# Second half of the channel weights converted in ScalarE's order behind channel items, and two passes for three batches instead of two

## The chip, the core and the metric

One core of a Trainium2 chip runs the whole program. TensorE (PE) multiplies, VectorE (DVE), ScalarE (ACT) and GpSimd (POOL) do elementwise work, SyncE (SP) issues the DMAs. Each engine takes its instructions in one fixed order and waits on semaphores where an operand is not ready. The metric is device time in microseconds (us), lower is better.

## What is computed

Attention with rotated q and k over 4 batches, 8 heads, 576 positions, then two mixing layers. The last layer (moe2) is the one the change touches:

```python
h = np.maximum(xt @ w_tok1, 0.0) @ w_tok2      # along the 576 positions
u = x + h.transpose(0, 2, 1)
h2 = np.maximum(u @ w_ch1, 0.0) @ w_ch2        # 512 -> 1536 -> 512 channels
return u + h2
```

The layer before it makes `x = sigmoid(xr @ w_r) * (relu(xk @ w_k)**2 @ w_v)`. The weights come as 64-bit floats, so each weight tile is first turned into 32-bit words on the chip and then split into a high and a low part; each product is three matmuls (high by high, high by low, low by high).

## The kernel before

The program has an order that a scheduler makes from priorities and from its own reckoning of when operands are ready; the order in which the source emits instructions is only its starting point. Three stages at the end matter here.

**Gates and tokens.** `gate_gen(b)` makes, for each batch and each half of 288 positions, four tiles `f` (DVE, L956) and splits them into `xs` (ACT and POOL), then sixteen groups of three matmuls into `rp`, a sigmoid `q` on ACT and a product `y` on POOL. `tok_gen(b)` transposes `y` into `trp`, copies it to `ytk` (high part on ACT, low part on DVE), multiplies by `w_tok1` into `t1p`, splits the result `h` and multiplies by `w_tok2` into `t2p`, which DVE adds to `y`. The tokens of the last batch (3) run beside the first channel items.

**Channels.** `ch_gen` works in *items*: one item is one tile of 128 of the 1536 channels for one half of one batch, so there are 8 chunks x 12 = 96 items. An item has 12 matmuls into `c1p`, a `hs` high part (ACT, relu with a scale), a float copy `ht` of the same (DVE, L1120), the low part `hs = ht - hs` (POOL, L109), and, two items later (`LAG = 2`), 12 matmuls into four accumulators `co`. Items of one chunk and one half of the channels make a run of `HALF = 6` items. `TWICE = 2` says that the first two batches (4 chunks) are done in two passes: first the lower six channel tiles of all four chunks (blocks with `hs = (0,)`), then the upper six (`(1,)`). The remaining chunks take both halves in one block (`(0, 1)`). At a block's end DVE empties the four `co` tiles (L1142), and for a first pass leaves the partial sum in `sums`. Before a block, `chain` finds its scale (DVE, with one matmul `mp` over the partitions) and `split` makes `uhl` from `u` (four times ACT L80 and DVE L1095).

**Weight conversion.** `Conv` takes weight tiles in pairs through four stages: DMA of `words`, `cv` on ACT (L213), three integer operations and a row maximum on DVE (L217, L218, L220, L225), and `parts`: high on ACT (L80 into `parts`), low on DVE (L238). `conv2` holds the lower half of `w_ch1` (8 tiles of 384 columns); `conv3`, here `cv3`, the upper half of `w_ch1` (8 tiles of 384) and the upper half of `w_ch2` (6 tiles of 512): 14 tiles, needed from the first `(1,)` block on. Its steps are emitted in the loop of the channel stage.

Of the kernel before, what the change touches and what calls it, by code (L numbers as in the profile page):

```python
# [7 lines left out]
F32 = mybir.dt.float32  # L8
# [4 lines left out]
ALU = mybir.AluOpType  # L13
# [21 lines left out]

KVN = 5

CW, HALF, TWICE = DCH // 2, KC // 2, 2

PACE, STEP, REST = (24, 28), 1, 8  # L40

# [28 lines left out]
def body(tc, kin, qin, vw, tabs, ident, mu, w_k, w_v, w_r, w_t1, w_t2, w_c1, w_c2, out):  # L70
# [41 lines left out]
    with ctx:  # L112
# [68 lines left out]
        class Conv:  # L181


            def __init__(self, cv, weights, name, load=None, low="P", room=None):
                self.cv, self.name, self.load, self.low, self.room = cv, name, load, low, room
                self.q = [(w, i) for w in weights for i in range(len(w.srcs))]
                if weights[-1].raw:
                    self.q[:0] = [None] * (len(self.q) % 2)
                self.n, self.words, self.t = 0, {}, {}
# [4 lines left out]
            def stage(self, j, i):  # L194
# [15 lines left out]
                if j == 1:  # L210
                    v = self.t[i] = self.cv()[:, :w]
                    x = hw if wide else self.words[i][:, :w]
                    act.activation(out=v.bitcast(F32), in_=x.bitcast(F32), func=AF.Copy, scale=REBIAS if wide else 1.0)  # L213
                elif j == 2 and wide:
                    v = self.t[i]
                    m = self.room()[:, :w] if self.room else v
# [792 lines left out]
        c2_b = c2_part(HALF, KC)  # L1009
        for nm, n in (("ytk", 1), ("h1", 2), ("uhl", 2), ("hs", 3), ("ht", 2), ("st", 2), ("top", 1)):  # L1010
            M[nm] = top("m_" + nm, n)
        cv, cv3 = Conv(cv_t, c1_w[:1], "conv2", low="D"), Conv(cv_t, [c1_w[1], c2_b], "conv3", low="D")
        def all_max(m):

            p = tps("mp")
# [16 lines left out]
        def ch_gen():  # L1032
# [12 lines left out]

            def part(i):
                b, c = chunks[blocks[i][0]]
                if b not in sums:
                    sums[b] = P["xT"].tile([128, KD, S + 1], F32, tag="xT", name="sums")
                return sums[b][:, :, c * HS:(c + 1) * HS]  # L1050

            def chain(i, k):

# [48 lines left out]
            for n in range(len(items) + LAG):  # L1102
                if n < len(items):
                    i, o, kf = items[n]
                    x = n // HALF
                    last_half = o == blocks[i][1][-1]
                    if kf == 0:
                        chain(i, 0)
                        chain(i, 1)
                        split(x)  # L1110
                    uhl = u16[i, o]
                    p = c1_p.tile([128, 512], F32, tag="c1", name="c1p")
                    for kk in range(KD):
                        mm3(p[:, 0:HS], c1_w[o][kk], kf, uhl[:, kk], kk == 0, kk == KD - 1)
                    j = HALF * o + kf - HALF * blocks[i][1][0]
                    g = tops[blocks[i][1]][1][:, j:j + 1]
                    h = M["hs"].tile([128, 2, HS], F16, tag="hs", name="hs")
                    f = M["ht"].tile([128, HS], F32, tag="ht", name="ht")
                    act.activation(out=h[:, 0], in_=p[:, 0:HS], func=AF.Relu, scale=g)  # L1119
                    dve.tensor_scalar(out=f, in0=p[:, 0:HS], scalar1=g, scalar2=0.0, op0=ALU.mult, op1=ALU.max)  # L1120
                    tt(LOW, h[:, 1], f, h[:, 0], ALU.subtract)
                    hs_of[n] = h
                    if last_half and kf in (0, 2):
                        chain(i + 1, kf // 2)
                    if kf == 4:
                        split(x + 1)
                    yield 12
                if n >= LAG:
                    i, o, kf = items[n - LAG]
                    h = hs_of.pop(n - LAG)  # L1130
                    begin, end = kf == 0 and o == blocks[i][1][0], kf == HALF - 1 and o == blocks[i][1][-1]
                    w, l = c2_at[HALF * o + kf]
                    for m in range(KD):
                        if begin:
                            co_of[m] = co_p.tile([128, 512], F32, tag="co", name="co")
                        mm3(co_of[m][:, 0:HS], w[l], m, h, begin, end)
                    if end:
                        e = row_of[i][:, 5 * KD + 3:]
                        final = blocks[i][1] != (0,)
                        for m in range(KD):  # L1140
                            u = cols(i)[:, m]
                            dve.scalar_tensor_tensor(out=u if final else part(i)[:, m], in0=co_of[m][:, 0:HS], scalar=e,  # L1142
                                                     in1=part(i)[:, m] if blocks[i][1] == (1,) else u, op0=ALU.mult,
                                                     op1=ALU.add)
                        if final:
                            b, c = chunks[blocks[i][0]]
                            sp.dma_start(out[b, c], cols(i))
                    yield 12

        n = 0  # L1150
        while B - 1 not in g_done or B - 2 not in u_done or not cv.done():
# [3 lines left out]
            n += 1  # L1155
            if n % STEP == 0 and not cv.done():
                cv.step()
        ch = Stream(ch_gen())
        ch.advance(1)
        tok.advance(8)  # L1160
# [5 lines left out]
        while not ch.done:  # L1166
            ch.advance(24)
            tok.advance(REST)
            n += 1
            if n % 2 == 0 and not cv3.done():  # L1170
                cv3.step()
        mx.close()
        mw.close()
# [63 lines left out]
```

## Time and profile before

| | us |
|---|---|
| median of 3 runs | 961.42 (959.79 to 962.22) |
| the profiled execution | 953.36 |
| its span, first to last instruction | 951.5 |
| PE busy over the span | 859.0 (90%) |
| DVE busy | 653.4 (69%) |
| ACT busy | 505.0 (53%) |
| POOL busy | 481.1 (51%) |

The span is measured on one execution with the hardware profiler; 1.9 us of its time lie outside the span. All stretches below are in us from the span's start.

### The profile page before, as it was taken

What the parts mean: (1) busy time and instruction counts of PE and PEld (TensorE: products, weight loads), DVE (VectorE), ACT (ScalarE), POOL (GpSimd) and SP (SyncE); (2) the same over time, 40 slices, a digit from 0 to 9 for tenths busy, and PEclk for the clock granted to TensorE, in tenths of its full rate; (3) what the DMA queues carried; (4) which work ended last, traced back from release to release, by engine and by line L of the source; (5) the groups of instructions that cost most, each with busy time, mean ns of one, the idle gap of its engine ahead of it and who ended that gap; (6) DMA issues with size and microseconds to landing.
All of it is one profiled execution on the core that took longest, in us unless ns stands there. A gap on an engine that the chain in (4) does not pass through costs nothing.

```text
span 951.5 us, 18563 instructions
## 1 busy us (share of the span) xinstructions
PE 859.0 (90%) x6870; PEld 751.6 (79%) x6870; DVE 653.4 (69%) x1471; ACT 505.0 (53%) x1121; POOL 481.1 (51%) x512
## 2 busy tenths in 40 slices
PE   3899988897887988997799899999999999999997
PEld 2889977776776877786699898897887888878876
DVE  5898578777698787784997899885545455344332
ACT  2787657767677777784556575653322223223221
POOL 7998568779677765352643354451122222222221
PEclk9999979899999999999999999999999999999999
DMA  8784268898799986889435634100000000000000
GB/s 266 228 273 152 83 138 188 166 198 190 180 173 183 202 164 137 149 169 297 172 120 174 192 118 139 45 2 1 1 1 2 25 26 26 26 25 2 25 26 25
DMA packets 167786, 112.05 MB, mean 118 GB/s; under 512 B 132368, under 2 KB 146832, under 8 KB 167184
## 3 DMA queue, kind: packets, MB, share of 16 engines
q1 hardware_dynamic: 167696, 110.87, 46.7%
q8 instruction: 54, 0.88, 0.4%
q14 instruction: 36, 0.29, 0.1%
HBM read 60.90 MB, written 14.16 MB: 79 GB/s over the span
## 4 chain that ended last, share of the span: by engine, by line
PE 42%; DVE 8%; ACT 3%; issue 2%; DMA 2%; POOL 1%; SPq 0%; DVEq 0%; ACTq 0%; POOLq 0%
PE c1p L712 5%; PE co L712 5%; PE c1p L713 5%; PE c1p L714 5%; PE co L713 5%; PE co L714 5%; DVE cv L218 2%; DVE cv L220 1%; DMA vd<-vt 1%; PE rp L713 1%; PE rp L714 1%; PE rp L712 1%; PE vp L712 1%; PE vp L713 1%; PE vp L714 1%
## 5 line engine op out<-in xcount | busy, mean ns | idle before, releaser
L109 POOL TENSOR_TENSOR hs<-ht,hs 128x288 f16<-128x288 f32 x96 | 71.3, 744 | 231.6 <-DVE ht L1120 195.3
L1119 ACT ACTIVATE hs<-c1p,top 128x288 f16<-128x288 f32 x96 | 47.8, 500 | 194.9 <-PE c1p L714 194.9
L1120 DVE TENSOR_SCALAR ht<-c1p,top 128x288 f32<-128x288 f32 x96 | 49.5, 516 | 119.3 <-ACT hs L1119 118.2
L444 DVE TENSOR_REDUCE nm<-S 128x1 f32<-128x576 f32 x144 | 104.0, 749 | 20.4 <-PE S L431 20.3
L714 PE MATMUL c1p<-uhl,parts 128*128 128x288 f16 x384 | 109.7, 286 | 0.0
L713 PE MATMUL c1p<-uhl,parts 128*128 128x288 f16 x384 | 109.7, 286 | 0.0
L712 PE MATMUL c1p<-uhl,parts 128*128 128x288 f16 x384 | 109.5, 286 | 0.0
L713 PE MATMUL co<-hs,parts 128*128 128x288 f16 x384 | 108.9, 286 | 0.0
L714 PE MATMUL co<-hs,parts 128*128 128x288 f16 x384 | 108.9, 286 | 0.0
L712 PE MATMUL co<-hs,parts 128*128 128x288 f16 x384 | 106.1, 286 | 0.4 <-ACT hs L1119 0.4
L712 PE MATMUL kp<-xs,parts 128*128 128x288 f32 x256 | 81.6, 324 | 21.5 <-ACT t L777 17.1
L431 PE MATMUL S<-kq 64*128 64x288 f32 (+1 forms) x696 | 75.9, 323 | 22.6 <-ACT kq L78 11.3
L712 PEld LDWEIGHTS <-parts 128*128 128x128 f16 x768 | 75.0, 98 | 19.4 <-issue 0.6
L713 PEld LDWEIGHTS <-parts 128*128 128x128 f16 x768 | 75.1, 98 | 19.0 <-issue 0.2
L714 PEld LDWEIGHTS <-parts 128*128 128x128 f16 x768 | 75.2, 98 | 18.9
L431 PEld LDWEIGHTS S<-kq 64*128 64x128 f32 (+1 forms) x696 | 60.1, 198 | 34.4 <-ACT kq L78 11.3
L109 POOL TENSOR_TENSOR q<-t 128x288 f32<-128x288 f32 x64 | 49.2, 771 | 74.2 <-ACT t L777 71.1
L713 PE MATMUL vp<-k,parts 128*128 128x288 f32 x256 | 78.8, 309 | 5.0 <-POOL k L109 4.9
L712 PE MATMUL vp<-k,parts 128*128 128x288 f32 x256 | 79.6, 314 | 4.0 <-ACT t L777 2.2
L713 PE MATMUL kp<-xs,parts 128*128 128x288 f32 x256 | 78.2, 306 | 0.3 <-POOL xs L109 0.2
L714 PE MATMUL vp<-k,parts 128*128 128x288 f32 x256 | 77.6, 304 | 0.0
L714 PE MATMUL kp<-xs,parts 128*128 128x288 f32 x256 | 77.5, 304 | 0.0
(154 smaller groups left out, 2478.3 us busy)
## 6 DMA issues: line engine op xcount, KB each, us to landing
rq<-in_qin_dram SPq DMA_DIRECT2D x30, 320.0 KB, 3.5
rk<-in_kin_dram SPq DMA_DIRECT2D x32, 288.0 KB, 3.3
words<-in_w_c_dram SPq DMA_DIRECT2D x12, 512.0 KB, 4.0
words<-in_w_c_dram SPq DMA_DIRECT2D x16, 384.0 KB, 3.4
vr<-in_vw_dram SPq DMA_DIRECT2D x16, 320.0 KB, 3.3
xd<-xT SPq DMA_DIRECT2D x16, 288.5 KB, 3.3
xT<-xd SPq DMA_DIRECT2D x4, 1154.0 KB, 5.7
vd<-vt SPq DMA_DIRECT2D x32, 144.0 KB, 2.9
```

Of the source, the lines that this page charges most:

```text
L109: return (pool if e == "P" else dve).tensor_tensor(o, a, b, op=op)
L218: yield lambda: dve.scalar_tensor_tensor(out=m, in0=hw, scalar=SIGN, in1=m, op0=ALU.bitwise_and, op1=ALU.bitwise_or)
L220: yield lambda: dve.scalar_tensor_tensor(out=v, in0=lw, scalar=29, in1=m, op0=ALU.logical_shift_right, op1=ALU.bitwise_or)
L431: o = pe.matmul(S_t[j][:, h, 0:HS], lhsT=a[l, 128 * m:128 * m + 128], rhs=b[l, h * HS:(h + 1) * HS], start=(n == 0), stop=(n == 2))
L444: dve.tensor_reduce(out=nm, in_=S_t[j][:, :, 0:HS], op=ALU.max, axis=AX.XY, negate=True)
L712: pe.matmul(p, lhsT=wh, rhs=t[:, 0], start=first, stop=False)
L713: pe.matmul(p, lhsT=wh, rhs=t[:, 1], start=False, stop=False)
L714: pe.matmul(p, lhsT=wl, rhs=t[:, 0], start=False, stop=last)
L1119: act.activation(out=h[:, 0], in_=p[:, 0:HS], func=AF.Relu, scale=g)
L1120: dve.tensor_scalar(out=f, in0=p[:, 0:HS], scalar1=g, scalar2=0.0, op0=ALU.mult, op1=ALU.max)
```

## The change

Four edits, all about `cv3` and the channel passes. `TWICE` becomes 3, so three batches (6 chunks) take two passes, the fourth one. `cv3` gets `after="hs"`: each of its ACT instructions `cv` (L213) is tied, in ACT's order and with no semaphore, behind the latest `hs` that was emitted. The loop steps `cv3` at each third turn, counted from the channel stage's start, in place of each second. And in `(0,)` blocks the float copy `ht` is made by ACT in place of DVE. The partial sums of the third batch lie in the buffers of `w_r`, whose use has ended.

```diff
--- before.py
+++ after.py
@@ -35,7 +35,7 @@
 
 KVN = 5
 
-CW, HALF, TWICE = DCH // 2, KC // 2, 2
+CW, HALF, TWICE = DCH // 2, KC // 2, 3
 
 PACE, STEP, REST = (24, 28), 1, 8
 
@@ -181,8 +181,8 @@
         class Conv:
 
 
-            def __init__(self, cv, weights, name, load=None, low="P", room=None):
-                self.cv, self.name, self.load, self.low, self.room = cv, name, load, low, room
+            def __init__(self, cv, weights, name, load=None, low="P", room=None, after=None):
+                self.cv, self.name, self.load, self.low, self.room, self.after = cv, name, load, low, room, after
                 self.q = [(w, i) for w in weights for i in range(len(w.srcs))]
                 if weights[-1].raw:
                     self.q[:0] = [None] * (len(self.q) % 2)
@@ -210,7 +210,10 @@
                 if j == 1:
                     v = self.t[i] = self.cv()[:, :w]
                     x = hw if wide else self.words[i][:, :w]
-                    act.activation(out=v.bitcast(F32), in_=x.bitcast(F32), func=AF.Copy, scale=REBIAS if wide else 1.0)
+                    o = act.activation(out=v.bitcast(F32), in_=x.bitcast(F32), func=AF.Copy,
+                                       scale=REBIAS if wide else 1.0)
+                    if self.after:
+                        behind(o, self.after)
                 elif j == 2 and wide:
                     v = self.t[i]
                     m = self.room()[:, :w] if self.room else v
@@ -1009,7 +1012,7 @@
         c2_b = c2_part(HALF, KC)
         for nm, n in (("ytk", 1), ("h1", 2), ("uhl", 2), ("hs", 3), ("ht", 2), ("st", 2), ("top", 1)):
             M[nm] = top("m_" + nm, n)
-        cv, cv3 = Conv(cv_t, c1_w[:1], "conv2", low="D"), Conv(cv_t, [c1_w[1], c2_b], "conv3", low="D")
+        cv, cv3 = Conv(cv_t, c1_w[:1], "conv2", low="D"), Conv(cv_t, [c1_w[1], c2_b], "conv3", low="D", after="hs")
         def all_max(m):
 
             p = tps("mp")
@@ -1045,9 +1048,12 @@
 
             def part(i):
                 b, c = chunks[blocks[i][0]]
-                if b not in sums:
-                    sums[b] = P["xT"].tile([128, KD, S + 1], F32, tag="xT", name="sums")
-                return sums[b][:, :, c * HS:(c + 1) * HS]
+                if b not in sums and b < 2:
+                    t = P["xT"].tile([128, KD, S + 1], F32, tag="xT", name="sums")
+                    sums[b] = [t[:, m] for m in range(KD)]
+                elif b not in sums:
+                    sums[b] = [wr.pool.tile([128, S], F32, tag=f"p{m}", name="sums") for m in range(KD)]
+                return [t[:, c * HS:(c + 1) * HS] for t in sums[b]]
 
             def chain(i, k):
 
@@ -1116,8 +1122,11 @@
                     g = tops[blocks[i][1]][1][:, j:j + 1]
                     h = M["hs"].tile([128, 2, HS], F16, tag="hs", name="hs")
                     f = M["ht"].tile([128, HS], F32, tag="ht", name="ht")
-                    act.activation(out=h[:, 0], in_=p[:, 0:HS], func=AF.Relu, scale=g)
-                    dve.tensor_scalar(out=f, in0=p[:, 0:HS], scalar1=g, scalar2=0.0, op0=ALU.mult, op1=ALU.max)
+                    last["hs"] = act.activation(out=h[:, 0], in_=p[:, 0:HS], func=AF.Relu, scale=g)
+                    if blocks[i][1] == (0,):
+                        act.activation(out=f, in_=p[:, 0:HS], func=AF.Relu, scale=g)
+                    else:
+                        dve.tensor_scalar(out=f, in0=p[:, 0:HS], scalar1=g, scalar2=0.0, op0=ALU.mult, op1=ALU.max)
                     tt(LOW, h[:, 1], f, h[:, 0], ALU.subtract)
                     hs_of[n] = h
                     if last_half and kf in (0, 2):
@@ -1139,8 +1148,8 @@
                         final = blocks[i][1] != (0,)
                         for m in range(KD):
                             u = cols(i)[:, m]
-                            dve.scalar_tensor_tensor(out=u if final else part(i)[:, m], in0=co_of[m][:, 0:HS], scalar=e,
-                                                     in1=part(i)[:, m] if blocks[i][1] == (1,) else u, op0=ALU.mult,
+                            dve.scalar_tensor_tensor(out=u if final else part(i)[m], in0=co_of[m][:, 0:HS], scalar=e,
+                                                     in1=part(i)[m] if blocks[i][1] == (1,) else u, op0=ALU.mult,
                                                      op1=ALU.add)
                         if final:
                             b, c = chunks[blocks[i][0]]
@@ -1155,6 +1164,7 @@
             n += 1
             if n % STEP == 0 and not cv.done():
                 cv.step()
+        n = 0
         ch = Stream(ch_gen())
         ch.advance(1)
         tok.advance(8)
@@ -1167,7 +1177,7 @@
             ch.advance(24)
             tok.advance(REST)
             n += 1
-            if n % 2 == 0 and not cv3.done():
+            if n % 3 == 1 and not cv3.done():
                 cv3.step()
         mx.close()
         mw.close()
```

What this does to the order. First VectorE in the gate and token stage, about the second half of the tokens of batch 0 (`h_8155` is that half's tile `h`). Before:

```order
L238 SCALAR_TENSOR_TENSOR parts<-cv,rows,parts 128x384 x2
L217 TENSOR_SCALAR cv<-cv 128x384
L956 SCALAR_TENSOR_TENSOR f<-xT,mu_s,a 128x288
L217 TENSOR_SCALAR cv<-cv 128x384
L218 SCALAR_TENSOR_TENSOR cv<-words,cv 128x384 x2
L220 SCALAR_TENSOR_TENSOR cv<-words,cv 128x384
L899 SCALAR_TENSOR_TENSOR h_8155<-t1p,h_8155 128x256
L220 SCALAR_TENSOR_TENSOR cv<-words,cv 128x384
L899 SCALAR_TENSOR_TENSOR h_8155<-t1p,h_8155 128x256
L225 TENSOR_REDUCE rows<-cv 128x1 x2
L231 TENSOR_TENSOR rows<-rows 128x1
```

and with the change, at the same place (L959 is L956 of before, L902 is L899):

```order
L109 TENSOR_TENSOR y<-t2p,y 128x288 x3
L959 SCALAR_TENSOR_TENSOR f<-xT,mu_s,a 128x288
L109 TENSOR_TENSOR y<-t2p,y 128x288
L109 TENSOR_TENSOR ytk<-trp,ytk 128x256 x2
L959 SCALAR_TENSOR_TENSOR f<-xT,mu_s,a 128x288
L109 TENSOR_TENSOR ytk<-trp,ytk 128x256 x2
L109 TENSOR_TENSOR yrm<-trp,yrm 64x256
L959 SCALAR_TENSOR_TENSOR f<-xT,mu_s,a 128x288
L902 SCALAR_TENSOR_TENSOR h_8155<-t1p,h_8155 128x256 x2
```

The conversion rows of `cv3` (L217 to L238) are gone from between the tiles `f`, `ytk`, `h` and `y` here, and so they are to the end of the gate and token stage.

Second ScalarE at the first channel items. Before, around the `hs` of the fourth to the ninth item:

```order
L898 ACTIVATE h_9122<-t1p 128x256
L1119 ACTIVATE hs<-c1p,top 128x288 x3
L78 ACTIVATE ytk<-trp 128x256 x2
L1119 ACTIVATE hs<-c1p,top 128x288
L78 ACTIVATE ytk<-trp 128x256 x2
L1119 ACTIVATE hs<-c1p,top 128x288
L78 ACTIVATE yrm<-trp 64x256
L1119 ACTIVATE hs<-c1p,top 128x288
L898 ACTIVATE h_9419<-t1p 128x256 x2
L1119 ACTIVATE hs<-c1p,top 128x288
```

with the change, from the fourth item's `hs` on (L1125 is `hs`, L1127 the new `ht`, L213 and L80 into `parts` are `cv3`):

```order
L1125 ACTIVATE hs<-c1p,top 128x288
L1127 ACTIVATE ht<-c1p,top 128x288
L1125 ACTIVATE hs<-c1p,top 128x288
L1127 ACTIVATE ht<-c1p,top 128x288
L213 ACTIVATE cv<-words 128x384 x2
L1125 ACTIVATE hs<-c1p,top 128x288
L1127 ACTIVATE ht<-c1p,top 128x288
L78 ACTIVATE ytk<-trp 128x256
L80 ACTIVATE parts<-cv,rows 128x384 x2
L78 ACTIVATE ytk<-trp 128x256
L1125 ACTIVATE hs<-c1p,top 128x288
```

Each item now has two ACT rows, and the conversion stands between the items: its first `cv` behind the fifth item's `ht`, its last `parts` behind the 26th item.

Third VectorE at the end of a first-pass block, where `co` is emptied. Before (first block):

```order
L109 TENSOR_TENSOR y<-t2p,y 128x288 x2
L1120 TENSOR_SCALAR ht<-c1p,top 128x288
L109 TENSOR_TENSOR ytk<-trp,ytk 128x256 x2
L1120 TENSOR_SCALAR ht<-c1p,top 128x288
L109 TENSOR_TENSOR ytk<-trp,ytk 128x256 x2
L1142 SCALAR_TENSOR_TENSOR sums<-co,st,y 128x288
L1120 TENSOR_SCALAR ht<-c1p,top 128x288
L1142 SCALAR_TENSOR_TENSOR sums<-co,st,y 128x288 x3
L109 TENSOR_TENSOR yrm<-trp,yrm 64x256
L1065 TENSOR_REDUCE st<-y 128x4
```

with the change (second block; L1151 is L1142 of before, L1071 is L1065, L220 to L241 are the conversion, L1101 is `uhl`):

```order
L109 TENSOR_TENSOR y<-t2p,y 128x288
L136 RECIPROCAL rows<-rows 128x1
L241 SCALAR_TENSOR_TENSOR parts<-cv,rows,parts 128x384 x2
L1151 SCALAR_TENSOR_TENSOR sums<-co,st,y 128x288 x3
L220 TENSOR_SCALAR cv<-cv 128x384
L1151 SCALAR_TENSOR_TENSOR sums<-co,st,y 128x288
L220 TENSOR_SCALAR cv<-cv 128x384
L221 SCALAR_TENSOR_TENSOR cv<-words,cv 128x384
L1071 TENSOR_REDUCE st<-y 128x4
L221 SCALAR_TENSOR_TENSOR cv<-words,cv 128x384
```

The `ht` rows are gone from VectorE in first-pass blocks, and the conversion rows stand between the block's own. On PE the matmuls up to the first `c1p` and those of the 96 items are the same in number; there are two `chain`s more, and the final blocks are as before.

## Rows read from the trace of the kernel before

**Rows 1.** Windows: gate and token stage, first 30 items, rest (columns named in front).

```profile
core 0: us, PE busy (x) PEld busy (x) DVE busy (x) ACT busy (x) POOL busy (x), PEclk, DMA share, GB/s
530.00:646.00 116.00, 106.41 (x789) 101.97 (x788) 102.77 (x236) 69.38 (x173) 53.91 (x60) 0.99 0.27 87
646.00:735.00 89.00, 89.00 (x724) 73.48 (x724) 45.92 (x115) 23.96 (x55) 17.72 (x24) 1.00 0.00 1
735.00:945.00 210.00, 209.60 (x1713) 167.72 (x1712) 88.03 (x210) 54.54 (x116) 53.58 (x72) 1.00 0.06 21
```

**Rows 2.** Windows inside the gate and token stage, same columns.

```profile
530.00:643.00 113.00, 105.06 (x779) 100.85 (x778) 100.12 (x223) 67.85 (x168) 53.91 (x60) 0.98 0.27 89
618.00:643.00 25.00, 24.93 (x197) 24.93 (x198) 20.51 (x47) 12.25 (x31) 12.04 (x13) 1.00 0.01 2
544.60:548.90 4.30, 4.21 (x20) 4.11 (x20) 2.55 (x7) 3.54 (x8) 2.08 (x3) 0.61 0.54 128
```

**Rows 3.** PE's waits from 525 to 660: us in total, times, longest.

```profile
PE t1p L894 <- DVE ytk L109: 2.4, 3, 1.8
PE rp L712 <- ACT xs L78: 2.4, 2, 1.8
PE trp L880 <- DVE ytk L109: 1.6, 1, 1.6
PE rp L713 <- POOL xs L109: 1.0, 2, 0.7
PE trp L880 <- DVE y L109: 0.9, 2, 0.7
PE rp L712 <- ACT vt L78: 0.5, 1, 0.5
```

**Rows 4.** Timeline of DVE before its tile `f` at 542.87 (start, duration).

```profile
540.00 0.94 DVE L217 TENSOR_SCALAR cv<-cv 128x384 int32<-128x384 int32 x1
540.86 1.16 DVE L220 SCALAR_TENSOR_TENSOR cv<-words,cv 128x384 int32<-128x384 int32 x1
541.94 0.55 DVE L218 SCALAR_TENSOR_TENSOR cv<-words,cv 128x384 int32<-128x384 int32 x1
542.41 0.54 DVE L225 TENSOR_REDUCE rows<-cv 128x1 f32<-128x384 f32 x1
542.87 0.51 DVE L956 SCALAR_TENSOR_TENSOR f<-xT,mu_s,a 128x288 f32<-128x288 f32 x1
```

**Rows 5.** Groups of instructions from 540 on: busy us, mean ns | idle before, releaser.

```profile
L109 POOL TENSOR_TENSOR hs<-ht,hs 128x288 f16<-128x288 f32 x96 | 71.3, 744 | 231.6 <-DVE ht L1120 195.3 <-DVE st L1067 25.6 <-DVE st L133 10.7
L1119 ACT ACTIVATE hs<-c1p,top 128x288 f16<-128x288 f32 x96 | 47.8, 500 | 194.9 <-PE c1p L714 194.9
L1065 DVE TENSOR_REDUCE st<-y 128x4 f32<-128x1152 f32 x12 | 16.1, 1350 | 0.3
L238 DVE SCALAR_TENSOR_TENSOR parts<-cv,rows,parts 128x384 f16<-128x384 f32 (+1 forms) x16 | 12.0, 779 | 1.9 <-ACT parts L80 1.9
L220 DVE SCALAR_TENSOR_TENSOR cv<-words,cv 128x384 int32<-128x384 int32 (+1 forms) x15 | 11.6, 790 | 0.1
L218 DVE SCALAR_TENSOR_TENSOR cv<-words,cv 128x384 int32<-128x384 int32 (+1 forms) x15 | 10.1, 694 | 0.0
L80 ACT ACTIVATE parts<-cv,rows 128x384 f16<-128x384 f32 (+1 forms) x16 | 9.6, 648 | 2.2 <-DVE rows L136 2.2
L225 DVE TENSOR_REDUCE rows<-cv 128x1 f32<-128x384 f32 (+1 forms) x15 | 8.8, 595 | 0.0
L217 DVE TENSOR_SCALAR cv<-cv 128x384 int32<-128x384 int32 (+1 forms) x14 | 8.0, 581 | 0.7 <-ACT cv L213 0.7
L1142 DVE SCALAR_TENSOR_TENSOR sums<-co,st,y 128x288 f32<-128x288 f32 x16 | 7.6, 512 | 4.4 <-PE co L714 4.4
L213 ACT ACTIVATE cv<-words 128x384 f32<-128x384 f32 (+1 forms) x13 | 7.5, 609 | 1.0 <-DVE parts L238 1.0
```

**Rows 6.** Groups of DVE from 646 to 735, the two costliest, same columns.

```profile
L1120 DVE TENSOR_SCALAR ht<-c1p,top 128x288 f32<-128x288 f32 x24 | 12.4, 515 | 25.2 <-ACT hs L1119 24.0 <-POOL hs L109 0.9 <-issue 0.3
L1095 DVE SCALAR_TENSOR_TENSOR uhl<-y,st,uhl 128x288 f16<-128x288 f32 x20 | 9.8, 537 | 1.8 <-ACT uhl L80 1.8
```

**Rows 7.** Tile `cv` from 547 to 640: ns min/median/max, first and last start.

```profile
L220 DVE SCALAR_TENSOR_TENSOR cv<-words,cv x13: 545/679/1170, 550.7 to 632.4; 128x384 int32<-128x384 int32 x7, 128x512 int32<-128x512 int32 x6
```

**Rows 8.** The chain that ended last, from 700 to 712: start, us, what.

```profile
704.71 0.22 PE mp L1016 x2
```

## The prediction

> **What bounds the kernel now.** I read the windows first, stage by stage. From 735 to 945 PE is busy for 209.60 of 210 us, and from 646 to 735 for all of 89 us [rows 1]: the channel stage is bound by PE, at 210/1713 = 0.1226 us for a matmul, so an item of 24 matmuls takes 2.94 us and a block of six 17.7 us. DVE is busy for 45.92 of those 89 us, ACT for 23.96 and POOL for 17.72, so there is free time on all three. The stage before it is another matter: from 530 to 646 PE is busy for 106.41 of 116 us while DVE is busy for 102.77 [rows 1]. DVE is the crowded engine there, and PE waits for what DVE makes.
>
> How much PE loses there I bound from two sides. From 530 to 643, just before the first channel item, PE is busy for 105.06 of 113 us, so 7.9 us are idle. Part of the busy time is slow too: from 544.60 to 548.90 the granted clock is 0.61 of full, mostly the lower level of 1.2 GHz, after PE had stood idle for some 2 us, and 20 matmuls take 4.30 us [rows 2]. From 618 to 643, where PE hardly ever stops, 197 matmuls take 25.00 us, 0.127 each. At that pace the 20 would take 2.5 us, so the clock costs 1.8 us. Idle and clock make 9.7 us, my lower bound on the loss. The upper one is by pace: 779 matmuls at 0.127 would take 98.9 us in place of 113, a loss of 14.1 us [rows 2]; it takes the mix of matmuls of those 25 us for that of the whole stage.
>
> The list of PE's waits says whom it waits for: DVE's `ytk` and `y` (2.4, 1.6 and 0.9 us), ACT's `xs` (2.4 us), POOL's `xs` (1.0 us), ACT's `vt` (0.5 us) [rows 3]. ACT's `xs` is itself late because of DVE: the tile `f` starts on DVE at 542.87, and 540.00 to 542.87 are filled with four conversion instructions [rows 4], two of which (the L217 at 540.00 and the L218 at 541.94) belong to the first tile of `cv3`.
>
> **The change part by part.**
>
> *Conversion leaves the gate and token stage.* By the groups from 540 on one converted tile costs DVE 0.581 + 0.694 + 0.790 + 0.595 + 0.779 = 3.44 us, and ACT 0.609 + 0.648 = 1.26 us [rows 5]. The 14 tiles of `cv3` make 48 us of DVE and 18 us of ACT. The rows of order show them gone from between `f`, `ytk`, `h` and `y`. DVE's load in 113 us falls from 100.12 [rows 2] to about 52. I let the change give back the lower bound of 9.7 us, less the waits that do not run through DVE (1.0 + 0.5) and 0.3 us for new ones: **-7.9 us**. The gain is at least about 4 us, should half the waits turn into waits for the chain `f`, `xs` on ACT, `xs` on POOL, which stays as it is; at most 14.1 us by pace. The wait of 1.6 us for `ytk` lies behind 643 (it is at the start of the channel stage) and is counted in none of these. DMA is no term: the loads of `xT` for batches 2 and 3 now stand in SP's queue ahead of most of the conversion's words instead of behind them, and nobody in the list waits for either.
>
> *Conversion enters the first pass.* It spans the 5th to the 26th item, 22 items or 65 us of PE, plus what is left of the tokens of batch 3. Take the stretch of 89 us from 646 to 735: DVE had 45.92 us [rows 1], loses the 24 `ht` (12.4 us) [rows 6], gains 48: 82 us, or 92% of it. That is as crowded as the gate and token stage was (100.12 of 113, 89%). ACT gets 24 x 0.500 for `ht` [rows 5] and 18 for the conversion: 23.96 + 12 + 18 = 54 of 89 us, which is no bound. What hides the 82 us is that an item no longer needs DVE: `hs` and `ht` are ACT's, the low part is POOL's, and `co` of an item comes two items (5.9 us) after its `c1p`. DVE's work is needed once per block: four `uhl` before it, four L1142 and the `chain` behind it. If that cover is gone, two queues matter. On ACT, `parts` waits for DVE's rows and the next item's `hs` stands behind it, so with two `c1p` buffers PE waits when ACT is held for more than some 3 us. On DVE, L1142 and `uhl` stand behind conversion rows, and the next block's first `co` or `c1p` waits for them. By block: two pairs of tiles (4 x 3.44), four `uhl` at 0.537 [rows 6], four L1142 at 0.512 and one L1065 at 1.350 [rows 5] make 13.8 + 2.1 + 2.0 + 1.4 = 19.3 us against PE's 17.7. These durations overlap a little from one instruction to the next, so the true load is nearer to PE's. Lower bound of the loss: 0, as in the same 89 us before, where PE lost nothing. Upper bound: the rate at which PE lost time beside an equally crowded DVE, 9.7 to 14.1 us in 113, over some 76 us: 6.5 to 9.5 us. I take **+3.0 us**, nearer to the lower end, for the items' independence of DVE.
>
> Here a row meets a rule. The longest L220 takes 1170 ns, the shortest 545 [rows 7], 0.6 us more, about one POOL instruction of 744 ns [rows 5]. In the first pass POOL works for 17.72 of 89 us against 53.91 of 116 in the stage before [rows 1], so the rows say that the conversion gets cheaper per tile by its move, not dearer. The Trainium skill (SBUF, "Who interferes with whom") says that a DVE instruction with two SBUF inputs contends with a GpSimd instruction that reads SBUF, and that the one that comes second is blocked fully rather than slowed. By it each of the 24 low parts could hold up a conversion row for its whole length, an estimate of 24 x 0.744 = 18 us more DVE load at the worst; 82 + 18 passes the 89 us by 11, and the sum would be -7.9 + 11 + 0.4 = +3.5 us, 964.9. By the rows it stays at the sum below.
>
> *Three batches in two passes.* Two blocks more: two `chain`s, whose `mp` matmuls take 0.22 us of PE each [rows 8]: **+0.4 us**. Eight L1142 more (4.1 us of DVE) and two L1065 (2.7 us) lie beside PE. `cv3` is done by the 26th item, and the first `(1,)` block begins with the 37th, so nothing waits for it. Before it began with the 25th, which with the conversion in this stage would have been too early; this edit and the ACT `ht` are there for the cover and cost no more. The blocks from there to the end, and the last output, are those of before.
>
> Sum: -7.9 + 3.0 + 0.4 = -4.5 us. On the profiled execution's own 953.36 us that is 948.9. The runs shown have a median 8.1 us above it, so the prediction is 961.4 - 4.5 = **956.9 us**.
>
> **Rivals.** (B) *The cover is complete.* The gate and token stage gives some 12 us, between its bounds, and PE never waits in the first pass, as it did not in these 89 us before [rows 1]: -12 + 0.4, 949.8 us. Against it: DVE's 19.3 us per block. (C) *The waits only move.* The gate and token stage stays bound by the chain through ACT and POOL and gives 4 us, the first pass takes 4: +0.4, 961.8 us. For it: POOL's own waits in the list; against it: ACT and POOL are busy for 69 and 54 of 116 us. (D) *DVE becomes the bound of the first pass.* ACT's `cv` and `parts` sit in order between items, so ACT follows DVE and PE follows ACT. With a loss of 9 us, near the upper bound, against a gain of 5: +4.4, 965.8 us. It decides from the point where DVE's work between two block ends exceeds PE's 17.7 us by more than the some 3 us of buffers; by clean durations it does not, by those of the crowded stage (19.3) it comes near within two blocks. That the change does nothing is excluded by the rows of order.
>
> **How the numbers follow.** Forecast 0.50 (its own range 953 to 960), B 0.14, C 0.22, D 0.14. The bound for faster or slower, 0.3%, about what a measurement here can tell from no change, is 2.9 us: 958.5 and 964.3. The forecast's slow edge falls under "same" and C is there too, B is faster, D slower with 0.14: faster 0.61, same 0.25, slower 0.14. The range of 8 in 10 takes B's price at one end and leaves out most of D at the other: 949.5 to 964.5.
>
> **What would show it.** Right: in the stage before the first `c1p`, DVE near 50% and PE idle for 2 to 4 us instead of 7.9, that `c1p` starting some 8 us earlier, no stretch at 0.61 of the clock near 545; in the 89 us behind it DVE near 90% and PE idle for about 3 us, in waits of `c1p` for `uhl` or of `co` for `sums`. Wrong: the first `c1p` hardly earlier, with PE waiting for POOL's `xs`; or a first pass in which PE waits for ACT's `hs` in most items while ACT waits for DVE's `rows`, each block taking 19 us or more.

## The result: faster, and by more than forecast

The changed kernel takes 947.94 us (median of four runs, 947.05 to 952.04) against 960.61 us for the kernel before (four runs, 956.73 to 962.22): a ratio of 0.9882 (taken over the runs, not of the two medians), 95% interval 0.984 to 0.9924. The forecast was 956.9 with 949.5 as the fast end of its range, so the direction was right and the size too small. The profiled execution spans 945.2 us, 6.3 less than before.

I cut the span at three marks that both programs have: the last matmul into `vp` (up to there the two programs issue the same instructions in the same order on every engine), the first into `c1p`, the last into `c1p`. The view of a tile gives them (start of the first and of the last). The changed kernel (L714 of before is L717 here, L712 is L715):

```profile
L717 PE MATMUL vp<-k,parts x256: 290/295/442, 174.3 to 534.6; 128*128 128x288 f32 x128
L715 PE MATMUL c1p<-uhl,parts x384: 286/286/297, 640.9 to 935.0; 128*128 128x288 f16 x192
L717 PE MATMUL c1p<-uhl,parts x384: 286/286/286, 641.3 to 935.3; 128*128 128x288 f16 x192
```

The same view of the kernel before:

```profile
L714 PE MATMUL vp<-k,parts x256: 290/295/445, 172.1 to 531.8; 128*128 128x288 f32 x128
L712 PE MATMUL c1p<-uhl,parts x384: 283/286/298, 647.2 to 941.3; 128*128 128x288 f16 x192
L714 PE MATMUL c1p<-uhl,parts x384: 283/286/296, 647.6 to 941.6; 128*128 128x288 f16 x192
```

The part that nobody changed ended 2.8 us later (534.6 against 531.8), which is within its spread between executions (last section). The gate and token stage went from 115.4 us (531.8 to 647.2) to 106.3 us (534.6 to 640.9): 9.1 us gained. The channel stage took 294.4 us (647.2 to 941.6) and takes 294.4 us (640.9 to 935.3): nothing lost, nothing gained. -9.1 + 2.8 = -6.3, the whole difference of the spans.

**Gate and token stage.** Between these marks, the kernel before (columns as in the first group of rows):

```profile
531.80:647.20 115.40, 105.81 (x785) 101.35 (x783) 102.25 (x237) 68.78 (x172) 53.91 (x60) 0.99 0.26 84
```

and the changed kernel, with the four microseconds after 546, then the first 89 us of the channel stage, the stretch from the first `cv` to the last `parts` of `cv3`, and the rest of the program:

```profile
534.60:640.90 106.30, 102.63 (x784) 101.03 (x783) 57.47 (x139) 54.91 (x144) 49.34 (x60) 0.98 0.13 43
546.00:550.00 4.00, 4.00 (x21) 3.91 (x20) 2.09 (x4) 2.54 (x6) 1.78 (x3) 0.61 0.11 42
641.00:730.00 89.00, 88.66 (x723) 73.13 (x723) 69.67 (x174) 46.21 (x105) 21.51 (x26) 1.00 0.19 59
656.00:733.90 77.90, 77.56 (x634) 63.63 (x632) 67.80 (x167) 41.88 (x94) 19.03 (x23) 1.00 0.22 67
740.00:935.00 195.00, 195.00 (x1596) 156.34 (x1594) 86.06 (x213) 52.13 (x112) 48.70 (x66) 1.00 0.06 22
```

PE has as many matmuls (784, 785). DVE falls from 102.25 us to 57.47, 54% of the stage. PE's idle time falls from 115.4 - 105.8 = 9.6 us to 3.7. The list of PE's waits in the stage, changed kernel, answers to [rows 3]:

```profile
PE trp L883 <- DVE ytk L109: 1.5, 1, 1.5
PE rp L716 <- POOL xs L109: 1.0, 1, 1.0
PE rp L715 <- ACT xs L78: 0.6, 1, 0.6
PE rp L715 <- ACT vt L78: 0.5, 1, 0.5
```

Of the waits of [rows 3], those of `t1p` for `ytk` (2.4 us) and of `trp` for `y` (0.9) are gone, ACT's `xs` costs 0.6 in place of 2.4; POOL's `xs`, ACT's `vt` and the last `ytk` stand as they were.

**First pass.** From 656.0 to 733.9 DVE is busy for 67.80 of 77.9 us, 87%, and PE idles for 0.34 us of them, in one wait. Of all waits of the changed kernel from 641 to 740, those that matter here:

```profile
ACT hs L1125 <- PE c1p L717: 33.1, 18, 4.5
ACT parts L80 <- DVE rows L136: 8.2, 4, 3.7
DVE cv L220 <- ACT cv L213: 3.5, 3, 2.3
PE co L715 <- ACT hs L1125: 0.3, 1, 0.3
```

ACT does stand still for DVE's `rows`, up to 3.7 us at a time, with `hs` behind it, as the prediction feared; but in 18 of the 30 items of this window ACT is ahead and waits for PE (33.1 us), and that lead takes the stall up: PE's one wait for `hs` is 0.3 us. DVE's conversion groups of the changed kernel, from 641 to 740, answer to [rows 5] (L217, L218, L220, L225, L238 of before are L220, L221, L223, L228, L241):

```profile
L223 DVE SCALAR_TENSOR_TENSOR cv<-words,cv 128x384 int32<-128x384 int32 (+1 forms) x14 | 9.5, 680 | 0.0
L241 DVE SCALAR_TENSOR_TENSOR parts<-cv,rows,parts 128x384 f16<-128x384 f32 (+1 forms) x14 | 9.0, 676 | 2.5 <-ACT parts L80 2.4
L221 DVE SCALAR_TENSOR_TENSOR cv<-words,cv 128x384 int32<-128x384 int32 (+1 forms) x14 | 8.6, 617 | 0.1
L228 DVE TENSOR_REDUCE rows<-cv 128x1 f32<-128x384 f32 (+1 forms) x14 | 8.2, 597 | 0.0
L220 DVE TENSOR_SCALAR cv<-cv 128x384 int32<-128x384 int32 (+1 forms) x14 | 6.3, 458 | 3.7 <-ACT cv L213 3.5
```

The same row operations cost 680 + 676 + 617 + 597 + 458 = 3028 ns a tile here, 3.03 us against 3.44 before. One of the five, the row maximum, did not change (597 and 595 ns).

### The profile page after: what moved, and what is told of

It reads as the page before. It is cut to its first block, busy times and chain, and to the rows that moved or that the text cites. A ratio compares the mean times of both kernels' runs of the same rounds, so it can differ in the third digit from the quotient of the medians.

```text
span 945.2 us, 18566 instructions
## 1 busy us (share of the span) xinstructions
PE 858.6 (91%) x6874; PEld 754.5 (80%) x6874; DVE 640.3 (68%) x1461; ACT 519.4 (55%) x1157; POOL 478.9 (51%) x512
## 4 chain that ended last, share of the span: by engine, by line
PE 49%; DVE 5%; DMA 4%; ACT 1%; issue 1%; SPq 1%; DVEq 0%; ACTq 0%
PE co L715 5%; PE c1p L715 5%; PE c1p L716 5%; PE c1p L717 5%; PE co L716 5%; PE co L717 5%; PE rp L715 2%; PE rp L716 2%; PE rp L717 2%; PE vp L715 1%; DMA pt<-p 1%; PE vp L716 1%; PE S L434 1%; PE vp L717 1%; DMA y<-vd 1%
## 5 line engine op out<-in xcount | busy, mean ns | idle before, releaser
L109 POOL TENSOR_TENSOR hs<-ht,hs 128x288 f16<-128x288 f32 x96 | 73.4, 765 | 229.5 <-DVE ht L1129 115.4
L1125 ACT ACTIVATE hs<-c1p,top 128x288 f16<-128x288 f32 x96 | 47.8, 498 | 161.6 <-PE c1p L717 161.6
L717 PE MATMUL c1p<-uhl,parts 128*128 128x288 f16 x384 | 109.7, 286 | 0.0
L715 PE MATMUL c1p<-uhl,parts 128*128 128x288 f16 x384 | 109.5, 286 | 0.0
L717 PE MATMUL co<-hs,parts 128*128 128x288 f16 x384 | 108.6, 286 | 0.0
L715 PE MATMUL co<-hs,parts 128*128 128x288 f16 x384 | 105.1, 286 | 0.3 <-ACT hs L1125 0.3
L715 PE MATMUL kp<-xs,parts 128*128 128x288 f32 x256 | 83.5, 332 | 20.2 <-ACT t L780 14.9
L715 PEld LDWEIGHTS <-parts 128*128 128x128 f16 x768 | 75.1, 98 | 19.3 <-issue 0.5
L717 PEld LDWEIGHTS <-parts 128*128 128x128 f16 x768 | 75.2, 98 | 18.6
L1129 DVE TENSOR_SCALAR ht<-c1p,top 128x288 f32<-128x288 f32 x60 | 30.9, 515 | 77.6 <-ACT hs L1125 77.6
L715 PE MATMUL vp<-k,parts 128*128 128x288 f32 x256 | 79.2, 312 | 4.4 <-ACT vt L78 2.6
L716 PE MATMUL vp<-k,parts 128*128 128x288 f32 x256 | 77.6, 304 | 5.3 <-POOL k L109 5.3
L716 PE MATMUL kp<-xs,parts 128*128 128x288 f32 x256 | 79.6, 312 | 0.6 <-POOL xs L109 0.6
L717 PE MATMUL kp<-xs,parts 128*128 128x288 f32 x256 | 78.7, 308 | 0.0
L717 PE MATMUL vp<-k,parts 128*128 128x288 f32 x256 | 76.4, 299 | 0.0
```

The lines of the kernel that those rows point to most:

```text
L109: return (pool if e == "P" else dve).tensor_tensor(o, a, b, op=op)
L715: pe.matmul(p, lhsT=wh, rhs=t[:, 0], start=first, stop=False)
L716: pe.matmul(p, lhsT=wh, rhs=t[:, 1], start=False, stop=False)
L717: pe.matmul(p, lhsT=wl, rhs=t[:, 0], start=False, stop=last)
L1125: last["hs"] = act.activation(out=h[:, 0], in_=p[:, 0:HS], func=AF.Relu, scale=g)
```

## The experiments

The theory was that the tie alone makes the gain in the gate and token stage, and that the first pass loses nothing because ACT's `ht` (and perhaps the third batch) leaves DVE out of the items. The rivals were that the passes or the ACT `ht` make the gain themselves; that the tie shifts something else; and, for the forecast's +3.0 us, that a crowded DVE costs PE in proportion to its load, or only from the point where it is full. Stage lengths below are between the marks above; a difference of the totals is never read without them, since the part before 531.8 varies from run to run (last section).

| | ratio to before, 95% | last `vp` at | gate and token stage | channel stage |
|---|---|---|---|---|
| before | | 531.8 | 115.4 | 294.4 |
| changed | 0.9882 (0.984 to 0.9924) | 534.6 | 106.3 | 294.4 |
| changed, again | 0.9931 (0.9905 to 0.9958) | 537.0 | 106.5 | 294.3 |
| changed, third time | 0.9901 (0.9865 to 0.9937) | 530.4 | 106.1 | 294.3 |
| no tie | 0.9964 (0.993 to 0.9998) | 534.5 | 115.6 | 293.9 |
| `ht` on DVE | 0.997 (0.9949 to 0.9992) | 537.3 | 106.1 | 300.0 |
| two batches | 0.9904 (0.9876 to 0.9933) | 538.4 | 106.1 | 294.9 |
| more DVE work, one dose | 0.9925 (0.9898 to 0.9952) | 535.4 | 106.4 | 298.2 |
| more DVE work, two doses | 1.008 (1.0047 to 1.0113) | 544.0 | 106.1 | 307.9 |
| tie alone | 0.9985 (0.9958 to 1.0011) | 540.1 | 106.1 | 301.7 |
| passes alone | 1.0011 (0.9982 to 1.004) | 534.0 | 116.4 | 293.9 |
| tie of `conv1` too | 0.9862 (0.9832 to 0.9893) | 525.5 | 110.9 | 294.3 |

**The changed kernel again**, unchanged, beside the other experiments.

> The changed kernel itself, once more, beside the kernel before. Theory 1 (the gain is what PE lost to the conversion in the gate and token stage, 9.0 us between the two traces, and the first pass costs nothing): ratio 0.989 to 0.992, that is 8 to 11 us. Theory 2 (a further gain of some 4 us outside that stage, since the medians stood 12.7 us apart): ratio 0.985 to 0.988. In the trace the time from the last vp matmul to the first c1p near 106 us against 115 before, under both.

> The changed kernel a third time, since its two comparisons so far gave 0.9882 and 0.9931 and the stages of the traces say 9.1 us, 0.9905. If the stages are the whole effect: ratio 0.987 to 0.994, the interval holding 0.9905; the last vp matmul at 532 to 540 us in its trace, wherever this execution's earlier part happens to end, and 106 and 294 us behind it. If there is more in the change than these two stages: below 0.987.

Measured: 950.03 against 957.70 us, and 948.19 against 958.98. The three comparisons give -12.7, -7.7 and -10.8 us; the gate and token stage gives -8.9 to -9.3 in all three, and the channel stage stands within 0.1 us. The second ratio, 0.9931, lies above both ranges expected of it, the third, 0.9901, in its range, with its last `vp` matmul 1.6 us ahead of the expected 532 to 540. The interval of the second (0.9905 to 0.9958) would hold the forecast of -4.5 us; those of the other two do not.

**No tie.** The third batch, the ACT `ht` and the rarer steps stay.

```diff
-Conv(cv_t, [c1_w[1], c2_b], "conv3", low="D", after="hs")
+Conv(cv_t, [c1_w[1], c2_b], "conv3", low="D")
```

> Everything of the change but the tie: the conversion's ACT rows are free, and the scheduler puts them back between the gates and tokens. Theory 1: the gain is gone, ratio 0.998 to 1.003, DVE again near 89% in the gate and token stage and PE idle there for 7 to 9 us. Rival (the gain comes from ht on ACT, from the passes or from the earlier xT loads): ratio near 0.99.

Measured: the gate and token stage is back at 115.6 us. Its window, and two of PE's waits in it (no tie):

```profile
534.50:650.10 115.60, 105.87 (x785) 101.38 (x783) 102.60 (x237) 69.10 (x173) 53.95 (x60) 0.99 0.26 84
```

```profile
PE t1p L897 <- DVE ytk L109: 2.4, 3, 1.8
PE rp L715 <- ACT xs L78: 2.4, 2, 1.8
```

DVE's 102.60 us stand where 102.25 stood, and the waits are those of [rows 3]. The total's interval ends just under 1, but neither stage shows a gain to go with it. What the order leaves free to run early fills DVE in the stage ahead, and the tie is what stops it. The tie also puts SP's loads of `xT` ahead of most of the conversion's words, in every kernel that has it, so no run takes the two apart; but the kernel before shows no wait of PE, DVE, ACT or POOL for a DMA between the marks, and DVE's `f`, which reads `xT`, waits only for POOL's `xs` (4.7 us).

**`ht` on DVE.** Tie, third batch and steps stay.

```diff
-                    if blocks[i][1] == (0,):
-                        act.activation(out=f, in_=p[:, 0:HS], func=AF.Relu, scale=g)
-                    else:
-                        dve.tensor_scalar(out=f, in0=p[:, 0:HS], scalar1=g, scalar2=0.0, op0=ALU.mult, op1=ALU.max)
+                    dve.tensor_scalar(out=f, in0=p[:, 0:HS], scalar1=g, scalar2=0.0, op0=ALU.mult, op1=ALU.max)
```

> The change with ht left on DVE in first-pass blocks. DVE then has 77 + 30 x 0.515 = 93 of the first 99 us of the channel stage. Theory 1 (cover is wide, items wait for nobody): PE loses 0 to 2 us there, ratio to the kernel before 0.989 to 0.993. Rival (cover was made by moving ht to ACT): PE loses 4 to 9 us in the first pass, ratio 0.993 to 1.0.

Measured: the gate and token stage keeps its gain (106.1), the channel stage loses 300.0 - 294.4 = 5.6 us, as the rival theory expected; theory 1, a wide cover, missed. The conversion's stretch, a part of it, PE's waits in the channel stage and one of POOL's (`ht` on DVE):

```profile
658.20:740.80 82.60, 78.78 (x625) 63.66 (x624) 77.23 (x188) 33.77 (x70) 19.21 (x22) 0.98 0.20 63
715.20:718.60 3.40, 3.40 (x17) 2.24 (x16) 2.72 (x8) 1.58 (x3) 0.00 (x0) 0.50 0.00 0
```

```profile
PE c1p L716 <- DVE uhl L1101: 1.7, 1, 1.7
PE co L716 <- POOL hs L109: 1.1, 1, 1.1
PE c1p L715 <- ACT uhl L80: 0.7, 1, 0.7
PE c1p L715 <- DVE ht L1126: 0.2, 1, 0.2
708.99 1.10 POOL L109 TENSOR_TENSOR hs<-ht,hs 128x288 f16<-128x288 f32 x1 [2.06 <-DVE ht L1126]
```

PE idles for 3.8 us of that stretch. Of its waits, those of `c1p` for `uhl` (1.7 and 0.7 us) are what the forecast had named for the changed kernel; they come when the cover is taken away. The other two run through `ht` (1.1 and 0.2 us): POOL's `hs`, which `co` waits for, started late because of it. From 715.2 to 718.6, behind the waits, the granted clock is 0.50, the lower of its two levels, and 17 matmuls take 3.40 us; at the prediction's 0.1226 us for a matmul they would take 2.1, so some 1.3 of the 5.6 us are the clock.

**Two batches in two passes**, tie and ACT `ht` kept, with the steps of before.

```diff
-CW, HALF, TWICE = DCH // 2, KC // 2, 3
+CW, HALF, TWICE = DCH // 2, KC // 2, 2
-            if n % 3 == 1 and not cv3.done():
+            if n % 2 == 0 and not cv3.done():
```

> The change with two batches in two passes as before, and the conversion stepped at each second item so that it ends in time. The 42 us of conversion on DVE must fit into some 18 items (53 us and the tokens of batch 3). Theory 1 with a limit at the DVE's full load: PE loses 3 to 8 us in the first pass or at the first block of the second pass, ratio 0.993 to 1.0. Rival (the third batch is not needed): no PE wait, ratio as the changed kernel's, 0.988 to 0.992.

Measured: 106.1 and 294.9, the changed kernel within 0.5 us. The conversion's stretch is shorter and denser (two batches):

```profile
659.60:725.40 65.80, 65.46 (x534) 53.80 (x532) 60.48 (x151) 37.08 (x82) 15.17 (x19) 1.00 0.25 79
```

DVE is at 60.48/65.8 = 92% and PE still idles for only 0.34 us. So the rival holds and the expected loss of 3 to 8 us missed: the third batch and the rarer steps are not needed.

**The tie alone**: both of the last two edits together, which leaves the kernel before plus the tie (and the step counter's fresh start).

> The kernel before with the tie alone: two batches in two passes, ht on DVE, the conversion stepped at each second item. The gate and token stage 106 us, as in the changed kernel. Theory 1a: the channel stage loses at least what ht on DVE lost (5.6 us), more as the conversion has fewer items: 300 to 306 us in place of 294, ratio to the kernel before 0.997 to 1.003. Rival (the tie is the whole change): 294 to 296 us, ratio 0.99.

Measured: 106.1 and 301.7: the tie gains 9.3 us in one stage and loses 7.3 in the next, and the total shows no difference. Beside two batches (294.9), which differs by `ht` on ACT alone, `ht` is worth 6.8 us here. The conversion's stretch (tie alone):

```profile
661.00:733.90 72.90, 69.39 (x558) 56.24 (x556) 70.08 (x171) 30.36 (x63) 15.24 (x19) 1.00 0.22 71
```

**The passes alone**: the kernel before with three batches in two passes, no tie, `ht` on DVE, the steps of before.

> The kernel before with three batches in two passes and nothing else. By the term of the sum 0.4 us more: the channel stage 294.3 to 295.2 us, the gate and token stage 115 to 116, ratio 0.997 to 1.003. If the partial sums of the third batch cost PE a wait at the blocks' ends: the channel stage 296 us or more.

Measured: 959.18 against 958.98 us; 116.4 and 293.9. Two `chain`s more cost nothing that these marks resolve. The gate and token stage is as in the kernel before (passes alone):

```profile
534.00:650.40 116.40, 106.34 (x786) 101.54 (x785) 102.34 (x237) 68.69 (x172) 54.29 (x60) 0.99 0.25 83
```

**More DVE work in the first pass.** The changed kernel, with two of the five conversion operations of each `cv3` tile issued once more (`range(1)`) or twice more (`range(2)`); the repeated operations give the same bits. By the rows above a dose is 14 x (617 + 680) ns = 18.2 us of DVE.

```diff
+                    for _ in range(1 if self.after else 0):
+                        yield lambda: dve.scalar_tensor_tensor(out=m, in0=hw, scalar=SIGN, in1=m, op0=ALU.bitwise_and,
+                                                               op1=ALU.bitwise_or)
+                        yield lambda: dve.scalar_tensor_tensor(out=v, in0=lw, scalar=29, in1=m,
+                                                               op0=ALU.logical_shift_right, op1=ALU.bitwise_or)
```

> The changed kernel with two of the conversion's DVE instructions of the 14 moved tiles issued twice (they give the same bits again): 28 more, some 18 us of DVE in the first pass, about 96 us of its first 100. Theory 1a (ht left on DVE cost 5.6 us because each item then stood behind conversion rows on DVE; load alone does little as long as the items need ACT and POOL only): the channel stage, first to last c1p, 294 to 297 us. Rival 1b (it was the load, and DVE at 87 of 100 us was already too much): 300 us or more.

> The same two instructions issued three times: some 36 us more on DVE in the first pass than in the changed kernel, 114 us of work for its first 100 us. Both theories: DVE is the bound now, the channel stage 305 to 320 us, and PE waits for hs while ACT waits for DVE's rows or parts. If it stays under 300 us, the conversion's place in ACT's order leaves more room than the sums of busy time say.

Measured: the channel stage takes 298.2 us (+3.8) and 307.9 us (+13.5). The first dose falls between the two theories: DVE is not full, yet PE loses. The conversion's stretch with one dose:

```profile
656.80:747.40 90.60, 87.27 (x705) 70.63 (x704) 84.76 (x206) 46.58 (x102) 23.10 (x26) 1.00 0.18 58
```

and with two doses, then the 50 us from 740 on, and PE's longest wait in the stage:

```profile
665.20:777.50 112.30, 107.74 (x859) 85.74 (x857) 106.72 (x242) 51.92 (x114) 28.45 (x32) 1.00 0.15 47
740.00:790.00 50.00, 42.78 (x323) 32.16 (x321) 43.47 (x102) 22.49 (x48) 10.69 (x14) 0.93 0.07 22
```

```profile
PE mp L1024 <- DVE st L1081: 4.8, 1, 4.8
```

With two doses the conversion runs so late that a block's `chain` stands behind it on DVE, and PE waits for `st` above all, not for `hs` as expected. In the 50 us shown PE idles for 7.2 us and the granted clock is 0.93, so a part of the 13.5 us is the clock.

Six kernels, one profiled execution each, give the share of DVE in the conversion's own stretch and the loss. With `ht` on ACT: 87% no loss, 92% 0.5 us, 93.5% (84.76/90.6) 3.8 us, 95% over 112 us 13.5 us. With `ht` on DVE: 93.5% (77.23/82.6) 5.6 us, 96% (70.08/72.9) 7.3 us. In these kernels PE begins to lose between 92 and 93.5%, a little below a full DVE, and then steeply; but the share does not stand apart from the loss, since a PE that waits makes the stretch longer. At the same 93.5% `ht` on DVE costs 1.8 us more than a dose of conversion does: PE's idle time is 0.5 us more (3.8 against 3.3), and some 1.3 us are the clock behind it.

**The tie in the stage ahead too.** In the kernel before and in the changed one, `kp` waits for ACT's `t` in the gated layer that runs beside `conv1`, in the part that the change left alone. Two of the waits of the kernel before from 425 to 490:

```profile
ACT cv L213 <- DVE parts L109: 9.2, 7, 2.3
PE kp L712 <- ACT t L777: 8.0, 6, 2.3
```

ACT's `cv` waits for DVE, and `t` seems to stand behind it: the same pattern. So `conv1` gets the same tie, behind `t`:

```diff
-                        act.activation(out=k2[m], in_=p[:, 0:HS], func=AF.Relu)
+                        last["t"] = act.activation(out=k2[m], in_=p[:, 0:HS], func=AF.Relu)
-        cv = Conv(cv_t, [wr, t1, t2, c2_part(0, HALF)], "conv1", low="D")
+        cv = Conv(cv_t, [wr, t1, t2, c2_part(0, HALF)], "conv1", low="D", after="t")
```

> The changed kernel with the same kind of tie for the conversion before: the ACT rows of conv1 (w_r, w_tok1, w_tok2 and the lower half of w_ch2) behind the latest t of the gated layer that was emitted. In the changed kernel PE waits 7.8 us for ACT's t between 425 and 490, and ACT's L213 waits 9.5 us there for DVE. If the mechanism carries over, most of these waits go: 3 to 7 us less than the changed kernel, ratio to the kernel before 0.984 to 0.989. Rival (the conversion has to be done by then and the waits move to the gates): as the changed kernel, 0.989 to 0.994.

Measured: from the last `pv` matmul to the last `vp` matmul, the stretch of that gated layer, 78.6 us against 86.3 in the kernel before and 86.5, 86.8 and 87.5 in the three profiles of the changed one. In the kernel before and then with both ties:

```profile
445.50:531.80 86.30, 75.90 (x542) 73.44 (x542) 78.11 (x144) 51.02 (x119) 39.70 (x45) 0.98 0.55 182
```

```profile
446.90:525.50 78.60, 74.22 (x543) 72.00 (x542) 55.11 (x104) 45.30 (x107) 42.08 (x45) 1.00 0.49 173
525.50:636.40 110.90, 103.66 (x785) 101.13 (x785) 76.19 (x182) 61.79 (x159) 51.25 (x60) 0.98 0.20 62
```

PE idles there for 4.4 us in place of 10.4, and the waits of `kp` for `t` from 425 to 490 come down to:

```profile
PE kp L715 <- ACT t L780: 3.0, 6, 0.6
```

DVE's 78.11 us fall to 55.11, but the work goes to the gate and token stage, where DVE rises from 57.47 to 76.19 us and the stage takes 110.9 us, 4.4 to 4.8 more than in the changed kernel. The net is some 3 to 4 us. 945.85 us (ratio 0.9862) is the lowest median measured and is clearly faster than before; against the changed kernel the stages say that it is ahead, the intervals of the totals overlap.

## Why the prediction was right and wrong

- **The stage and the mechanism.** Right. DVE, filled with conversion, was what PE waited for, and the order behind `hs` removes it: with the tie the stage takes 106.1 to 106.5 us in eight profiles, without it 115.4 to 116.4 in three.
- **-7.9 us for it.** Mis-sized; it measured -9.1, well inside its bounds. Its idle part was forecast at 7.9 - 1.5 - 0.3 = 6.1 us and measured 9.6 - 3.7 = 5.9. The other 3.2 us came from busy time (105.81 to 102.63 us for the same matmuls), where I had let only the 1.8 us of the slow clock come back. The clock is not what came back: in the changed kernel a stretch at 0.61 of full, mostly at the lower level of 1.2 GHz, still stands at 546 to 550, behind two waits of 0.99 and 0.56 us, and the repeats, whose stage shows a clock of 1.00 throughout, are as long (106.5 and 106.1 us). "No stretch at 0.61" was wrong for the first profile, right for those two. The traces say where the 3.2 us lie. Summed from each matmul's start to the next one's, the time before `t1p` falls by 4.4 us, before `rp` by 3.0 and before `trp` by 1.7, together the 9.1; before `t2p` it stands (19.07 and 19.10 us). One matmul of each of these takes as long as before, within 8 ns. So the matmuls overlap more: beside the waits that are listed, the same tiles lost shorter gaps between two starts, which do not show as idle time because the matmul before still counts as busy.
- **+3.0 us for the first pass.** This is the step that failed: it measured 0.0. Two things were wrong in it. The load was too high: in the 89 us from 641 to 730 DVE is busy for 69.67 us, not 82. A tile costs 3.03 us and not 3.44 (14 x 0.41 = 5.7 us), and some 1.4 us of the conversion lie behind the 89 us; the rest is not broken down, but durations that are added up count their overlaps twice, as the prediction says. And the price was taken from the wrong place: I carried over the rate at which PE lost time beside a DVE at 89% in the gate and token stage. The share does not set that rate: at 87% the first pass loses nothing and at 92%, with two batches, 0.5 us. That this is because no item needs DVE fits the waits (in the gates PE waits for DVE's `ytk` and `y`, in the first pass for one `hs` of ACT), but it is shown in part only. With `ht` on DVE the pass loses 5.6 us, yet that puts 9.4 us more on DVE as well (77.23 against 67.80), and one dose, which is load alone (17.0 us more, 84.76 against 67.80), brings back nearly as much idle time (3.3 against 3.8 us). Rival B, the complete cover, describes what happened in the first pass. That its 949.8 us is near the medians of 947.94 to 950.03 is luck in part: its 12 us for the stage before measured 9.1.
- **+0.4 us for the two `chain`s.** Not seen: 293.9 us with the passes alone, 294.4 before.
- **"This edit and the ACT `ht` are there for the cover."** True of `ht`, 5.6 us. Not true of the third batch: with two batches PE idles no more, so the conversion was not too late for the first `(1,)` block.
- **The rule of the Trainium skill** (SBUF — State Buffer, "Who interferes with whom"), that a DVE instruction with two SBUF inputs contends with a GpSimd instruction that reads SBUF. By the prediction's estimate it would at its worst have made the sum +3.5 us; nothing here shows that worst case. The conversion's tiles became cheaper beside a POOL that was busy for 24% of the time (19.03 of 77.9 us) than they were beside one at 47% (53.91 of 115.4). That they became cheaper is in line with contention; no run here varied POOL alone.
- **The absolute number.** Of the 9.0 us between 956.9 and 947.94 the terms explain 3.0 + 1.2 + 0.4 = 4.6, and the kernel before, 960.61 in place of the 961.4 of three runs, 0.8. The other 3.6 lie in neither stage, since the medians stand 12.7 us apart and the stages 9.1, and their cause stays open; the repeats, at 7.7 and 10.8 us, do not show them again. The kernel before measured 957.7 to 959.0 in the later comparisons; -4.5 would have been 953 to 954.5.

## What to carry to other kernels

Work that an order leaves free runs as early as it can and crowds the engine that the next stage waits for; tying it, by order alone, behind an instruction of a later stage moves it to where that engine has room, and the tie must come with whatever frees the path there (here `ht` on ACT: the tie alone gained 9.3 us and gave back 7.3). Before pricing a crowded engine, read from the list of waits whether each step of the critical engine needs it, or only each block: about 90% cost 9 us in one stage and at most 0.5 in the other. Even there the room ends a little below a full engine. And cut the spans of two kernels at marks that both have: here the stages told 9 us to a few tenths, when the totals said anything from 7.7 to 12.7.

## What was not expected of the hardware

Up to the last `vp` matmul every kernel here but the one with both ties runs the same program, yet that matmul started between 530.4 and 544.0 us in eleven profiled executions, a spread of 13.6 us. The spread lies ahead of the last `pv` matmul, and 11.1 us of it ahead of the first `vp` (172.1 to 183.2 us): from the last `pv` to the last `vp` the eleven took 86.3 to 88.9 us. Behind it the stage repeats to within 1 us (106.1 to 106.5 with the tie, 115.4 to 116.4 without). What makes the early part vary stays open.

PE lost time before DVE was full: at 93.5% of the conversion's stretch it already idled for 3.3 us of 90.6 with one dose. ACT and DVE, each with its fixed order, wait for each other there (from 641 to 745 `parts` for `rows` 7.0 us, `cv` for `parts` 0.2), and such a pair seems to give less than either alone; that reading is argued, not measured.
